# One-hot rows on GpSimd, the last gate product on VectorE and three more early folds there, in a kernel of pooled attention and a top-1 mixture of experts

## The chip, the cores and the metric

The kernel runs on one core of a Trainium2 chip. The time is the device time of one execution in microseconds; of several runs the median is taken. The engines of the core are TensorE (PE in the profile; its weight loads are listed apart as PEld), VectorE (DVE), ScalarE (ACT), GpSimd (POOL) and SyncE (SP, which issues most DMAs). Each works through its own list of instructions in a fixed order and waits at semaphores for the others.

## The reference

Keys and values are averaged over blocks of 8 rows, attention runs over the 72 pooled rows, and its output goes to a top-1 mixture of 8 experts. The shapes are q, k, v of 8 x 8 x 576 x 64; 4608 tokens of width 512; w1 of 8 x 512 x 1024 and w2 of 8 x 1024 x 512; all in float32.

```python
k_p = k.reshape(B, H, Sp, 8, D).mean(axis=3)
v_p = v.reshape(B, H, Sp, 8, D).mean(axis=3)
attn = softmax(q @ k_p.T / sqrt(D))            # + 1e-9 in the denominator
x = (attn @ v_p).transpose(0, 2, 1, 3).reshape(4608, 512)
logits = x @ w_gate + modality_bias[modality_id]
e_idx = argmax(logits); probs = exp(logits - max) / (sum(exp(logits - max)) + 1e-9)
out[t] = probs[t, e_idx] * (relu(x[t] @ w1[e_idx]) @ w2[e_idx])
```

## The kernel before

**Two stages.** The attention (lines 239 to 1059) works through 20 steps, five for each pair of batches: two steps of two 128-token tiles for the even batch, one step of one tile that mixes the leftover 64 tokens of both batches, and two steps for the odd one. That makes 36 tiles, in four groups of 9. The experts follow: tokens are sorted by expert into slots of 256, and each slot runs the two matrix products of its expert. The order on every engine is written out by hand, in the loop over `n` from line 978: what the loop calls first stands first in an engine's list.

**Folding.** A load brings the raw rows of a batch: `k_b` (four chunks of 128 blocks and a rest `k4` of 64) and `v_b` (four pairs of heads and a rest `v4`). Summing the 8 rows of a block is called folding here. GpSimd folds with three additions that halve the width (`fold`, lines 351 to 353); VectorE can fold one chunk with one reduction (`reduce8`, line 356). The results are `kp` and `vp`. TensorE then transposes `kp` (`pk`, line 396; ScalarE copies it to `kt`, lines 404 and 405) and `vp` (`pv`, lines 443 and 444).

**The gate.** The logits of the gate are linear in the values, so 8 extra columns of the value operand `vw` carry `v_p @ w_gate` (`v_gate`, lines 459 to 466): three products on TensorE, two copies by ScalarE, and for the rest `vp4` a copy `vg4` by ScalarE (line 465) and a product with a mask by GpSimd (line 466). The head part of that rest, line 438, is also GpSimd's.

**A step.** TensorE makes the scores `sc` (line 601, or 595 for a mixed tile); VectorE takes their maximum (`mx`, 608) and subtracts it (`sb`, 611); ScalarE takes the exponential (`pe`, 623 and 624). In the next step TensorE transposes the weights (`pp`, 630; the rest in line 642, into a free corner of a score bank) and multiplies them with the values (`a_pe`, lines 665 and 669, into `av`, which has one buffer). VectorE divides by the row sums (`x_dve`, lines 688 to 698: `r`, `lg`, `xb`), and `av` is free again. SP stores `xb` to `xs` in DRAM.

**Routing.** After each group, `route(g)` makes a list of small VectorE operations: logits `lgr`, their maximum, the exponentials `ex` (by ScalarE, 755), the one-hot choice `oh` (760), the sum `sm` of `ex` (777), plus 1e-9 (778), its reciprocal `gate` (782); then a count on TensorE (`pe`, 767 to 771), from which VectorE works out each token's rank, `rk`, `rki`, `rkm`, `rkf`, `rh` (800 to 805), and a row `arow` for each tile, which compares 0 to 127 with the rank (807). The list is dripped: `gap` pops one or two operations between those of a step. The operations that TensorE runs are held back and released once in a step. After group 1, `early_table` multiplies the 18 rows `arow` of groups 0 and 1 with `b0` (line 858, the product) and gets the list of tokens for the first two slots, which GpSimd gathers (line 144). The last group's operations are spread over the first slots of the experts by the table `late` (line 1202).

What order does at the head of a step is told by these lines:

```python
loads(n)
run(hook_0, n)                 # pool_v / pool_k of a coming batch, route
if old: t_pe(old[0]); t_act(old[0]); s_act(n, 0)
s_pe(n, 1)
if due: release()              # one held operation
...
run(hook_1, n)                 # k_operand, v_operand
a_pe(old[0])
s_dve(n, 1)
```

Below, `k_5` means the key rows of batch 5, and "group 1's sum" means the operation `sm` of `route(1)`.

## Time and profile before

| | |
|---|---|
| median of 3 runs | 590.27 us (589.53 to 592.23) |
| the profiled execution | 593.54 us, of which the span is 591.8 us |
| granted clock of TensorE | 0.998 of full |
| TensorE, VectorE, ScalarE, GpSimd busy over the span | 571.0, 370.2, 273.9, 191.8 us |
| folds on GpSimd, lines 351 to 353 | all before 138 us |
| one-hot rows on VectorE, line 807 | 36, between 85.6 and 196.1 us |

All times inside the execution count from the start of the span. A row of the timeline has the start, the busy time, the engine and line, the operation, what it writes and reads, the shapes, how many were merged, and in brackets how long the engine sat idle just before and what ended that. The view of windows lists for a stretch the busy time of PE, PEld, DVE, ACT and POOL (with the number of instructions), the granted clock, the share of the DMA engines and the rate in GB/s. The experts begin at about 184 us.

### The profile page before, as it was taken

The page shows a single profiled execution, that of the slowest core. Times are in us where ns is not written, and L with a number is a line of the kernel's source. Part 1 is how long each engine was busy: PE and PEld are TensorE (multiplying, and loading weights), DVE is VectorE, ACT ScalarE, POOL GpSimd, SP SyncE. Part 2 cuts the span into 40 slices and gives each one's busy share as a digit, 9 for nine tenths or more (in the row PEclk, how much of TensorE's full clock was granted, in tenths as well). Part 3 has the DMA queues.
Part 4 walks back from the last instruction along what each step waited for, and adds up shares of the span by engine and source line. Part 5 has one row for each costly group of instructions (what it writes and reads, how often), then busy time and mean ns, then how long its engine had stood idle before and what let it go on. Part 6 is the DMA issues. An engine that isn't in the chain of part 4 may idle for free.

```text
span 591.8 us, 12343 instructions
## 1 busy us (share of the span) xinstructions
PE 571.0 (96%) x3539; PEld 498.7 (84%) x3539; DVE 370.2 (63%) x941; ACT 273.9 (46%) x653; POOL 191.8 (32%) x300
## 2 busy tenths in 40 slices
PE   4899999999999999999999999999999999999996
PEld 4789889889898888888888888888888888888894
DVE  5757888789876865566455456865455487555311
ACT  2657757788652233334333336633343474334210
POOL 6689996855100233012012112022112113112101
PEclk9999999999999999999999999999999999999999
DMA  8999979994411653332232278232234843241001
GB/s 244 276 336 278 361 235 306 321 314 133 126 56 39 218 210 100 101 112 88 89 113 88 89 225 258 91 118 87 84 122 134 249 168 104 85 148 57 38 3 55
DMA packets 83426, 92.60 MB, mean 156 GB/s; under 512 B 17871, under 2 KB 58319, under 8 KB 83344
## 3 DMA queue, kind: packets, MB, share of 16 engines
q1 hardware_dynamic: 77424, 72.24, 39.4%
q0 software_dynamic: 5920, 19.44, 9.8%
q8 instruction: 30, 0.49, 0.3%
q14 instruction: 52, 0.43, 0.3%
HBM read 123.06 MB, written 27.58 MB: 255 GB/s over the span
## 4 chain that ended last, share of the span: by engine, by line
PE 79%; DMA 7%; DVE 6%; POOL 2%; ACT 2%; issue 2%; SPq 1%; POOLq 0%; DVEq 0%; ACTq 0%
PE op L1335 33%; PE hp L209 20%; PE hp L214 10%; DMA k<-in_k_dram 5%; PE av L665 3%; PE hp L183 3%; PE sc L601 2%; PE av L669 2%; PE ph L183 1%; PE pq L576 1%; PE pp L630 1%; DMA out_dram<-obw,slw 1%; DVE mx L608 1%; DVE hl L141 1%; DVE sb L611 1%
## 5 line engine op out<-in xcount | busy, mean ns | idle before, releaser
L209 PE MATMUL hp<-xhl,hl 128*128 128x512 f32 x512 | 126.6, 389 | 0.0
L1311 POOL DMA_INDIRECT out_dram<-ob,sidx x34 | 36.9, 1084 | 264.0 <-DVE ob L1305 191.5
L209 PEld LDWEIGHTS hp<-xhl,hl 128*128 128x128 f32 x512 | 96.0, 188 | 19.9
L217 ACT COPY ht<-hp 128x256 f32<-128x256 f32 x128 | 47.4, 373 | 139.2 <-PE hp L214 109.9
L218 DVE TENSOR_TENSOR ht<-ht,hp 128x256 f32<-128x256 f32 x128 | 52.7, 420 | 92.0 <-ACT ht L217 83.0
L1335 PE MATMUL op<-hl,hx 128*128 128x512 f32 x429 | 104.7, 392 | 0.0
L1335 PEld LDWEIGHTS op<-hl,hx 128*128 128x128 f32 x429 | 78.4, 188 | 14.6
L1335 PE MATMUL op<-hl,hh 128*128 128x512 f32 x256 | 79.8, 393 | 0.0
L214 PEld LDWEIGHTS hp<-xhl,hl 128*128 128x128 f32 x512 | 69.8, 190 | 4.9
L214 PE MATMUL hp<-xhl,hl 128*128 128x256 f32 x512 | 71.5, 282 | 0.0
L1335 PEld LDWEIGHTS op<-hl,hh 128*128 128x128 f32 x256 | 45.9, 189 | 7.9
L665 PE MATMUL av<-vw,pt 128*128 128x146 f32 (+1 forms) x320 | 49.3, 293 | 1.2 <-DVE xb L698 1.1
L1335 PE MATMUL op<-hl,hlo 128*128 128x512 f32 x128 | 49.8, 389 | 0.0
L144 POOL DMA_INDIRECT xg<-xs,gidx x36 | 38.7, 1074 | 29.0 <-DMA raw<-in_moe_w_dram 13.8
L665 PEld LDWEIGHTS av<-vw,pt 128*128 128x128 f32 (+1 forms) x320 | 39.7, 180 | 3.3 <-DVE xb L698 0.9
L223 DVE SCALAR_TENSOR_TENSOR hx<-ht,hx 128x256 fp32r<-128x256 f32 x64 | 27.1, 425 | 20.4 <-DVEq L1340 15.9
L223 DVE SCALAR_TENSOR_TENSOR hlo<-ht,hh 128x256 fp32r<-128x256 f32 x64 | 27.7, 434 | 18.1 <-DVEq L1340 13.7
L601 PE MATMUL sc<-kt,qt 128*128 128x144 f32 x256 | 37.4, 289 | 1.2 <-ACT qt L582 1.0
L601 PEld LDWEIGHTS sc<-kt,qt 128*128 128x128 f32 x256 | 33.1, 190 | 2.2 <-ACT qt L582 0.9
L608 DVE TENSOR_REDUCE mx<-sc 128x8 f32<-128x576 f32 (+1 forms) x40 | 27.7, 692 | 8.1 <-PE sc L601 6.0
L669 PE MATMUL av<-vw,pt 128*128 128x146 f32 (+1 forms) x160 | 30.1, 290 | 0.3 <-ACT pt L649 0.2
L611 DVE TENSOR_TENSOR sb<-sc,mx 128x576 f32<-128x576 f32 (+1 forms) x40 | 27.7, 693 | 2.4 <-DVE mx L608 0.6
(279 smaller groups left out, 906.5 us busy)
## 6 DMA issues: line engine op xcount, KB each, us to landing
raw<-in_moe_w_dram SPq DMA_DIRECT2D x288, 256.0 KB
xs<-xb SPq DMA_DIRECT2D x16, 528.0 KB
scr<-xg SPq DMA_DIRECT2D x29, 256.0 KB
k<-in_k_dram SPq DMA_DIRECT2D x7, 1024.0 KB
v<-in_v_dram SPq DMA_DIRECT2D x7, 1024.0 KB
q<-in_q_dram SPq DMA_DIRECT2D x7, 1024.0 KB
y<-scr SPq DMA_DIRECT2D x108, 64.0 KB
v<-in_v_dram SPq DMA_DIRECT2D x16, 128.0 KB
```

The costliest lines, as they stand in the source:

```text
L144: nc.gpsimd.indirect_dma_start(out=x, out_offset=None, in_=xs[0:rows, :], in_offset=IndirectOffsetOnAxis(idx[:, col:col + 1].bitcast(U32), 0),
L209: nc.tensor.matmul(hp[g % 2], hl[g][:, 0, d * P:(d + 1) * P], ab[:, d, :, 0:SLOT], start=(d == 0), stop=False)
L214: nc.tensor.matmul(hp[g % 2][:, 0:SLOT], hl[g][:, 1, d * P:(d + 1) * P], ab[:, d, 0, 0:SLOT], start=False, stop=(d == ND - 1))
L217: nc.scalar.copy(hts[g % 2], hp[g % 2][:, SLOT:2 * SLOT])
L218: nc.vector.tensor_add(hts[g % 2], hts[g % 2], hp[g % 2][:, 0:SLOT])
L223: nc.vector.scalar_tensor_tensor(hlo, hts[g % 2], 0.0, hh.bitcast(F32), op0=ALU.max, op1=ALU.subtract)
L601: nc.tensor.matmul(dst, qt[:, i, :], kt[b % NB][:, :, h * SPL:(h + 1) * SPL], start=True, stop=True)
L608: nc.vector.reduce_max(mx, scv, axis=AX.X)
L665: nc.tensor.matmul(av[hs, u, 2 * VC * gg:2 * VC * (gg + 1)], pt[:, c, hs], vw[y][:, c].rearrange("p a x -> p (a x)"), start=(gg == 0), sto ...
L669: nc.tensor.matmul(dst4[hs], pt4[:, hs], v4[y][:, 2 * u:2 * u + 2, :], start=False, stop=True)
L1311: nc.gpsimd.indirect_dma_start(out=out[:, :], out_offset=IndirectOffsetOnAxis(idx.bitcast(U32), 0), in_=ob, in_offset=None, bounds_check=N ...
L1335: nc.tensor.matmul(ot, l[:, ts_], hl[f][:, w, D:2 * D], start=(f == 0 and n == 0), stop=(f == NF - 1 and n == 2))
```

## The change

Five edits:

- **Rows.** GpSimd makes all `arow` rows. A list `onehot` takes those of groups 0 to 2; five of them are issued at the head of a step, ahead of that step's folds. The early product (`joins`) isn't released while rows are left. Group 3's go to GpSimd in the table `late`.
- **Gate product.** `v_gate`'s last product is done by VectorE straight from PSUM; ScalarE's copy `vg4` is gone.
- **Folds.** `k_1` chunk 3 moves later on VectorE; `v_1` chunk 2 and `k_2` chunks 2 and 3 go from GpSimd to VectorE.
- **Order.** In steps 1 and 2 the products `a_pe` move ahead.
- **Sum.** `ex` has a ninth column with 1e-9, set by a GpSimd memset when `route` is called, so that the sum contains it; the addition of line 778 is gone.

```diff
@@ pool_k / pool_v
-                        elif b > 1 or c < 2:
+                        elif b > 2 or c < 2:
                             fold(t[:, c:m], kp[:, c:m])
...
-            elif b:
+            elif b == 2:
                 fold(t[:, 2], vp[:, 2])
-            else:
+            elif b == 0:
                 fold(t[:, 2], vp[:, 2])
                 reduce8(t[:, 3, :], vp[:, 3, :])
...
-        def pool_k_rest(b):
-            reduce8(kraw[b][:, 3, :], kps[b][0][:, 3, :])
+        def pool_k_rest(b, c=3):
+            reduce8(kraw[b][:, c, :], kps[b][0][:, c, :])
...
-        def pool_v_rest(b):
-            reduce8(vraw[b][:, 3, :], vps[b][0][:, 3, :])
+        def pool_v_rest(b, c=3):
+            reduce8(vraw[b][:, c, :], vps[b][0][:, c, :])
@@ v_gate
-            vg4 = ap.tile([P, NPAIR, E], F32, tag="vg4", bufs=1, name=f"vg4_{b}")
-            nc.scalar.copy(vg4, pg[:, 2, :].rearrange("p (j e) -> p j e", j=NPAIR))
-            nc.gpsimd.tensor_tensor(d4[:, :, HD:HD + E], vg4, m4b.to_broadcast([P, NPAIR, E]), op=ALU.mult)
+            nc.vector.tensor_tensor(d4[:, :, HD:HD + E], pg[:, 2, :].rearrange("p (j e) -> p j e", j=NPAIR),
+                                    m4b.to_broadcast([P, NPAIR, E]), op=ALU.mult)
@@ release
-            if drip and drip[0] in held:
+            if drip and drip[0] in held and not (drip[0] in joins and onehot):
                 drip.pop(0)()
+        def some_rows(n):
+
+            for _ in range(min(n, len(onehot))):
+                onehot.pop(0)()
@@ route
-            ex = small("ex", g, [P, n, E])
+            ex = small("ex", g, [P, n, E + 1])
+            nc.gpsimd.memset(ex[:, :, E:E + 1], 1e-9)
...
-                nc.scalar.activation(ex, lg, AF.Exp)
+                nc.scalar.activation(ex[:, :, 0:E], lg, AF.Exp)
...
-            add(lambda: V.tensor_scalar_add(sm, sm, 1e-9))
...
-            for i in range(n):
-                add(lambda i=i: V.tensor_scalar(arow[:, t0 + i, :], iota_b, rkf[:, i:i + 1], None, op0=ALU.is_equal))
+            rows = [lambda i=i: nc.gpsimd.tensor_scalar(arow[:, t0 + i, :], iota_b, rkf[:, i:i + 1], None, op0=ALU.is_equal)
+                    for i in range(n)]
+            if g == len(GROUPS) - 1:
+                ops += rows
+            else:
+                add(lambda: onehot.extend(rows))
@@ early_table
             held.update((count, product))
+            joins.add(product)
@@ the loop over the steps
             loads(n)
+            some_rows(5)
             run(hook_0, n)
...
+            if n == 2:
+                a_pe(old[0])
             run(hook_1, n)
-            if old:
+            if old and n != 2:
                 a_pe(old[0])
             if has:
                 s_dve(n, 1)
-            if n == 1:
-                pool_k_rest(1)
...
+            if n == 1:
+                pool_k_rest(1)
+                pool_v_rest(1, 2)
+                a_pe(old[1])
+                x_dve(old[1])
+            if n == 2:
+                pool_k_rest(2, 2)
             if nxt:
                 s_pe(n + 1, 0)
...
+            if n == 2:
+                pool_k_rest(2)
...
-            if two:
+            if two and n != 1:
                 a_pe(old[1])
-            if two:
                 x_dve(old[1])
...
-        while drip:
+        while drip or onehot:
+            some_rows(GT)
@@ late
-        (0, 0): [lr[9], lr[7], lr[11], lr[8]],
-        (0, 1): [lr[10]],
-        (0, 3): [counts, lr[12]] + [fn for pair in zip(bases, lr[13:20]) for fn in pair] + lr[20:25],
+        (0, 0): [lr[8], lr[7], lr[10]],
+        (0, 1): [lr[9]],
+        (0, 3): [counts, lr[11]] + [fn for pair in zip(bases, lr[12:19]) for fn in pair] + lr[19:],
...
-        (0, 5): lr[25:] + columns,
+        (0, 5): columns,
```

**TensorE in step 1.** Before, the transposes of `kp` of batch 1 (`pk`) are followed by the scores of step 2, which read them, and only then by the value products of the second tile of step 0 (`av`):

```order
L396 MATMUL pk_0_490<-ident,kp_409 64x128 x3
L595 MATMUL sc_0_506<-kt_132,qt_0_481 64x144
L595 MATMUL sc_0_506<-kt_133,qt_0_481 64x144
L595 MATMUL sc_0_506<-kt_132,qt_0_481 64x144
L595 MATMUL sc_0_506<-kt_133,qt_0_481 64x144
L396 MATMUL pk_1_516<-ident,kp_409 64x128
L401 MATMUL pk_1_516<-ident,kp_1_410 64x64
L665 MATMUL av_521<-vw_136,pt_479 128x146 x2
L669 MATMUL av_521<-vw_138,pt_1_135 128x2x73
```

In the changed kernel the same place reads:

```order
L396 MATMUL pk_0_484<-ident,kp_407 64x128 x3
L670 MATMUL av_502<-vw_136,pt_473 128x146 x2
L674 MATMUL av_502<-vw_138,pt_1_135 128x2x73
L670 MATMUL av_502<-vw_136,pt_473 128x146 x2
L674 MATMUL av_502<-vw_138,pt_1_135 128x2x73
L600 MATMUL sc_0_515<-kt_132,qt_0_475 64x144
L600 MATMUL sc_0_515<-kt_133,qt_0_475 64x144
```

The four value products now stand between the transposes and their reader.

**GpSimd after group 0.** Before, the end of the folds of `v_4` is followed by the folds of `k_5`:

```order
L351 TENSOR_TENSOR v_4_758<-v_4_758 128x256
L352 TENSOR_TENSOR v_4_758<-v_4_758 128x128
L353 TENSOR_TENSOR vp_4_1232<-v_4_758 128x64
L351 TENSOR_TENSOR k_756<-k_756 128x2x256
L352 TENSOR_TENSOR k_756<-k_756 128x2x128
L353 TENSOR_TENSOR kp_1350<-k_756 128x128
```

Now:

```order
L351 TENSOR_TENSOR v_4_748<-v_4_748 128x256
L352 TENSOR_TENSOR v_4_748<-v_4_748 128x128
L353 TENSOR_TENSOR vp_4_1218<-v_4_748 128x64
L811 TENSOR_SCALAR arow<-iota_b,rkf_1011 128x128 x5
L351 TENSOR_TENSOR k_746<-k_746 128x2x256
L352 TENSOR_TENSOR k_746<-k_746 128x2x128
```

Five rows of group 0, which read VectorE's `rkf`, stand ahead of the folds of `k_5`; the other four stand ahead of the folds of `v_5`.

**GpSimd at group 1's sum.** Before, the folds of `k_6` end, the two products for the value operand of batch 5 follow, then the folds of `v_6`:

```order
L351 TENSOR_TENSOR k_6_1145<-k_6_1145 64x256
L352 TENSOR_TENSOR k_6_1145<-k_6_1145 64x128
L353 TENSOR_TENSOR kp_6_1591<-k_6_1145 64x64
L438 TENSOR_TENSOR vw_139<-vp_5_1482,m_142 128x4x64
L466 TENSOR_TENSOR vw_139<-vg_5_1719,m_142 128x4x8
L351 TENSOR_TENSOR v_995<-v_995 128x2x256
```

Now:

```order
L351 TENSOR_TENSOR k_6_1131<-k_6_1131 64x256
L352 TENSOR_TENSOR k_6_1131<-k_6_1131 64x128
L353 TENSOR_TENSOR kp_6_1575<-k_6_1131 64x64
L740 MEMSET ex_1589 128x9
L438 TENSOR_TENSOR vw_139<-vp_5_1466,m_142 128x4x64
L351 TENSOR_TENSOR v_983<-v_983 128x2x256
```

The memset of the ninth column, which group 1's sum on VectorE waits for, stands behind all folds of `k_6`. Group 0's stands in the same way behind those of `k_4`.

More of the change, by code (lines that the diff above doesn't have):

```diff
@@ L541 @@
                 tile_group[t] = (g, t - t0)
-        drip, held, stores = [], set(), []
+        drip, held, stores, onehot = [], set(), [], []
         def gap(n=2):
@@ L550, in release @@
         def release():
-            if drip and drip[0] in held:
+            if drip and drip[0] in held and not (drip[0] in joins and onehot):
                 drip.pop(0)()
+        def some_rows(n):
+            for _ in range(min(n, len(onehot))):
+                onehot.pop(0)()
+        joins = set()
         spare, pt4s = {}, {}
```

## The prediction

> **What bounds the kernel now.** I read the page first: TensorE is the busiest engine by far, so the question is where it isn't busy. The view of windows tells that (the first number after the stretch is its length, the second PE's busy time):
>
> ```profile
> 20.00:50.00 30.00, 27.28 (x221) 23.71 (x221) 20.68 (x45) 20.25 (x58) 23.96 (x41) 1.00 1.03 293
> 50.00:112.00 62.00, 60.45 (x506) 55.58 (x505) 51.86 (x155) 42.30 (x120) 52.61 (x91) 1.00 0.98 316
> 112.00:184.00 72.00, 69.92 (x610) 65.19 (x609) 56.94 (x171) 50.76 (x128) 22.70 (x35) 1.00 0.47 152
> 184.00:576.00 392.00, 392.00 (x2063) 336.22 (x2062) 226.49 (x548) 152.44 (x333) 76.60 (x77) 1.00 0.38 121
> ```
>
> From 184 us to 576 us TensorE is busy for 392.00 of 392 us, with the clock at 1.00, and the change takes nothing from its work. So the experts can neither gain nor lose, as long as every operand is there in time. Between 20 and 184 us 2.72, 1.55 and 2.08 us are missing: 6.35 us is all that a change to the attention can win behind the first loads. The timeline of TensorE names its waits; these seven rows are those that the edits touch, or that limit them (times from the span's start, in brackets the idle time and what ended it):
>
> ```profile
> 27.63 0.70 PE L595 MATMUL sc<-kt,qt 128*64 128x144 f32 x6 [0.65 <-ACT kt L405]
> ...
> 33.23 0.30 PE L444 MATMUL pv<-ident,vp 128*64 128x128 f32 x1 [0.81 <-POOL vp L353]
> ...
> 45.72 0.60 PE L576 MATMUL pq<-ident,q 128*128 128x128 f32 x4
> ...
> 48.67 0.30 PE L443 MATMUL pv<-ident,vp 128*128 128x128 f32 x1 [0.47 <-DVE vp L356]
> ...
> 86.99 0.30 PE L642 MATMUL sc<-ident,pe 128*128 128x128 f32 x1 [0.49 <-DVE sb L611]
> ...
> 124.70 0.30 PE L642 MATMUL sc<-ident,pe 128*128 128x128 f32 x1 [0.49 <-DVE sb L611]
> ...
> 165.90 0.66 PE L630 MATMUL pp<-ident,pe 128*128 128x128 f32 x4 [0.54 <-DVE h L187]
> ```
>
> The reader should see three kinds. Early on TensorE waits for `kt`, which is made from `kp`, and for folded values (`vp`), first from GpSimd, then from VectorE. At 86.99 and 124.70 it waits for a VectorE that is busy with one-hot rows of groups 0 and 1. At 165.90 it waits for VectorE among the rows of group 2. The row at 45.72, the transposes of the first queries of `q_2`, has no wait now; it matters below. In all, 0.65 + 0.81 + 0.47 + 0.49 + 0.49 + 0.54 = 3.45 us.
>
> **First term, 20 to 50 us.** The moved value products fill the wait at 27.63; with one fold less and no gate product ahead, GpSimd has `vp4` ready for 33.23. So TensorE comes up to 1.46 us earlier to 45.72. There the load of `q_2` stops it:
>
> ```profile
> 34.37 1.27 POOL L351 TENSOR_TENSOR k<-k 128x512 f32<-128x512 f32 x1 [1.20 <-DMA k<-in_k_dram]
> ...
> v<-in_v_dram SPq DMA_DIRECT2D x1, 1024.0 KB
> k<-in_k_dram SPq DMA_DIRECT2D x1, 1024.0 KB
> q<-in_q_dram SPq DMA_DIRECT2D x1, 1024.0 KB
> v<-in_v_dram SPq DMA_DIRECT2D x2, 128.0 KB
> k<-in_k_dram SPq DMA_DIRECT2D x1, 128.0 KB
> ...
> 34.37:45.72 11.35, 11.06 (x99) 10.06 (x97) 6.80 (x19) 5.97 (x17) 10.56 (x18) 1.00 1.06 335
> ```
>
> `k_2` lands at 34.37, since the fold that waits for it starts then. Behind it in SP's order lie a `k4` of 128 KB, a `v` of 1024, two halves of `v4` of 128 each, a `k` of 1024, and then `q_2` with 1024: 3456 KB, or 3.54 MB. The stretch moves 335 GB/s with the DMA engines full (share 1.06), so they take 10.56 us and `q_2` lands at 34.37 + 10.56 = 44.93, a bit less if the first bytes overlapped `k_2`. TensorE can't win more than 45.72 - 44.93 = 0.8 us there. Meanwhile VectorE, whose scores for step 4 stand ahead of those transposes, catches up, and the wait of 0.47 at 48.67 goes: **+1.3 us** by 50 us. The edits cost VectorE folds:
>
> ```profile
> 36.93 0.73 POOL L351 TENSOR_TENSOR k<-k 128x256 f32<-128x256 f32 x1
> ...
> 40.16 0.72 POOL L351 TENSOR_TENSOR k<-k 64x256 f32<-64x256 f32 x1
> ...
> 73.18 0.61 POOL L438 TENSOR_TENSOR vw<-vp,m 128x256 f32<-128x256 f32 x1
> ...
> L466 POOL TENSOR_TENSOR vw<-vg,m 128x32 f32<-128x32 f32 x8 | 1.9, 237 | 11.5 <-ACT vg L465 11.5
> ...
> L342 POOL MEMSET wgb<- 128x64 f32 x1 | 0.1, 149 | 0.0
> ...
> 47.46 1.07 DVE L356 TENSOR_REDUCE vp<-v 128x64 f32<-128x512 f32 x1
> ...
> 71.08 0.21 DVE L777 TENSOR_REDUCE sm<-ex 128x9 f32<-128x72 f32 x1
> ```
>
> A fold by VectorE takes 1.07 us. Three are new (the fourth is only moved), and VectorE is busy for 20.68 of 30 us in that window. The one that waits for `k_2` at 34.37 has only the maxima of step 3 behind it, for which the scores come later. So I cost them at nothing; without that cover each would cost up to its 1.07.
>
> **Second term, 50 to 75 us.** GpSimd folds without a pause from 34.37 to the row at 73.18. Two chunks of `k_2` go (36.93 to 40.16: 3.23 us), and two gate products at 0.2. So what stood at 73.18 stands at 69.5, and just there stands now the memset of group 0's ninth column. A memset of 64 columns took 149 ns: done at 69.7. Group 0's sum stood at 71.08 on VectorE, with the 1.3 us won at 69.8. The memset is just in time; more than 71.08 - 69.7 = 1.4 us can't be kept at this place. The addition that goes and the gate product that comes on VectorE are both small here and I set them against each other: **0**.
>
> **Third term, 75 to 112 us.** GpSimd's new rows need a price, and no row of the trace shows one. The nearest:
>
> ```profile
> L352 POOL TENSOR_TENSOR k<-k 128x128 f32<-128x128 f32 x12 | 5.5, 456 | 0.9
> ...
> L523 POOL TENSOR_SCALAR mq<-mf 128x36 f32<-128x36 f32 x2 | 0.6, 312 | 0.1
> ...
> L499 POOL TENSOR_SCALAR_AFFINE_SELECT tri<-tri 128x128 bf16<-128x128 bf16 x1 | 0.3, 292 | 0.1
> ```
>
> Two inputs of the same 128 columns take 456 ns, a bf16 operation with one input 292, the same operation with 36 columns 312. I take 0.35 us a row, nearest to the one-input rows, with 0.29 and 0.46 as the ends. [...]
>
> VectorE loses two rows ahead of the `sb` that TensorE waits for at 86.99: +0.5. But GpSimd now waits for VectorE's `rkf` before the folds of `k_5`, and everything behind them is late. When is `rkf` ready?
>
> ```profile
> 83.64 0.72 DVE L802 TENSOR_SCALAR rkm<-rki 128x9 int32<-128x9 int32 x1
> ...
> 84.47 0.44 DVE L804 CAST rkf<-rkm 128x9 f32<-128x9 int32 x1
> ...
> 163.28 0.17 DVE L802 TENSOR_SCALAR rkm<-rki 128x9 int32<-128x9 int32 x1
> ...
> 163.56 0.16 DVE L804 CAST rkf<-rkm 128x9 f32<-128x9 int32 x1
> ```
>
> Before, it ended at 84.91. In group 2, with GpSimd idle, the same `rkm` and `rkf` took 0.17 and 0.16 us in place of 0.72 and 0.44; GpSimd will stand still here. So 84.91 - 0.83 - 1.3 = 82.8. From there GpSimd has nine rows, the folds of `k_5` (as long as those of `k_6`), line 438 at 0.6, the folds of `v_5` and of `k_6`, and then group 1's memset:
>
> ```profile
> 93.27 1.27 POOL L351 TENSOR_TENSOR v<-v 128x512 f32<-128x512 f32 x1
> ...
> 100.09 1.27 POOL L351 TENSOR_TENSOR k<-k 128x512 f32<-128x512 f32 x1
> ...
> 107.49 0.61 POOL L438 TENSOR_TENSOR vw<-vp,m 128x256 f32<-128x256 f32 x1
> ...
> 108.64 0.22 DVE L777 TENSOR_REDUCE sm<-ex 128x9 f32<-128x72 f32 x1
> ```
>
> That is 7.40 + 0.6 + 6.82 + 7.40 + 0.15 = 22.4 us and nine rows: the memset is done at 82.8 + 22.4 + 3.15 = **108.3**. Group 1's sum stood at 108.64 and would now come at 106.8. It waits 1.5 us, with the maxima, `sb` and `x_dve` of step 12 queued behind it, and TensorE behind those. What is left at this point is 108.64 - 108.3 = 0.3, in general 3.5 us minus nine times the price: 0.9 at 0.29, -0.6 at 0.46.
>
> **Fourth term, 112 to 140 us.** The wait of 0.49 at 124.70 goes with group 1's rows: +0.5. But the early product now stands one step earlier, right behind the count at 133.08, and needs group 1's last four rows:
>
> ```profile
> 121.35 0.72 DVE L803 TENSOR_SCALAR rki<-rki 128x9 int32<-128x9 int32 x1
> 121.98 0.16 DVE L804 CAST rkf<-rkm 128x9 f32<-128x9 int32 x1
> ...
> 133.08 0.17 PE L852 MATMUL sc<-cum,ones 128*128 128x8 bf16 x1
> ```
>
> `rkf` ended at 122.14; 0.55 less for `rki` (GpSimd idle then) and 0.3 won: 121.3. Behind it are nine rows, the folds of `k_7` and line 438: 121.3 + 3.15 + 8.0 = 132.4. TensorE arrives at 133.08 - 0.8 = 132.3: no wait at 0.35, but 1.2 us at 0.46. The folds of `v_7`, the gathers and group 2's memset follow; GpSimd is busy for only 22.70 of 72 us in this window, which hides them.
>
> **Fifth term.** The rows of group 2 leave VectorE:
>
> ```profile
> 164.44 0.41 DVE L807 TENSOR_SCALAR arow<-iota_b,rkf 128x128 bf16<-128x128 bf16 x2
> ```
>
> Two of them, 0.4 us, stood ahead of the operation that TensorE waits for at 165.90: +0.3 of 0.54. Group 3's rows go from VectorE to GpSimd in the first slot, where TensorE is full in both: 0. The wider sum and the exponentials written with a gap I cost at nothing to 0.05 each. SP's load of the first expert's index moves ahead of `q_5`'s load; its input comes earlier too: 0.
>
> **Sum:** 1.3 won by 50 us, cut to 0.3 at 112, + 0.5 + 0.3 = **1.1 us** off the profiled execution's 593.54 (its span 591.8 and 1.7 around): 592.4. That execution is 3.3 us above the median of the runs, 590.27; carried over, **589.2**.
>
> **The rivals.**
>
> *GpSimd becomes the bound (slower).* Same mechanism, place 108.64 and 133.08, dearer row. At 0.41 us a row the third term is -0.2, the product waits 0.7, and -0.2 + 0.5 - 0.7 + 0.3 = -0.1: from there on the kernel is slower. At 0.46 it is -0.6 + 0.5 - 1.2 + 0.3 = -1.0 us, 591.3. For it speaks that every fold of GpSimd behind 82.8 is a two-input row at full price; against it the row of 292 ns. [...] Chance 0.25.
>
> *The waits go and nothing takes their place (faster).* If `rkf` comes sooner or a row costs well under 0.29, the sum of group 1 doesn't wait, and of the 3.45 us above all but the capped part goes: 1.3 + 0.5 + 0.5 + 0.3 = 2.6 us, 587.7; with the rest of the touched waits 3.4 us, 586.9. Chance 0.25.
>
> *Hidden anyway.* TensorE's 0.8 us before `q_2` doesn't come, since ScalarE's copies behind the transposes end last, and group 1 takes back the rest: -0.3 to 0.3, 590.3. Chance 0.1.
>
> **How the numbers follow.** The forecast has 0.4 and its own range is 588.3 to 590.0. With the rivals' ends 586.9 to 591.8 (0.5 beyond the dear row, as the product may wait for more), which leaves out 2 in 10 with the scatter of the runs. 0.5%, about what a measurement of this kernel can tell from no change, is 2.95 us: under 587.3 lies half of the faster rival and a little, 0.17; over 593.2 the tail of the slower one, 0.07; between them 0.76.
>
> **What would show it.** Right, if in the changed kernel TensorE's first queries of `q_2` wait for their DMA near 44.9; the waits for `kt` at 27.63 and for `vp` at 33.23 and 48.67 are gone; GpSimd idles for some 5 us until about 82.8 with VectorE's `rkf` as the releaser; VectorE waits for GpSimd at group 1's sum near 108.3; and the waits at 86.99 and 124.70 are gone. Wrong, if rows on GpSimd take over 0.41 us or under 0.29, if `q_2` lands earlier than 44, or if TensorE in step 12 doesn't follow VectorE so closely that a late sum delays it.

## The result, and the profile after

The changed kernel is slower: 597.06 us (594.82 to 600.67, 8 runs) against 592.1 us of the kernel before beside it (8 runs), a ratio of 1.0093 with a 95% interval of 1.0071 to 1.0115. (A ratio is estimated from the single runs, so it need not be the quotient of the two medians.) The forecast was 589.2 us, and its range ended at 591.8.

First the second profile of the kernel before (taken with the experiments below), since the first one was a late execution. The rows are from TensorE's timeline: the transposes of the first queries of `q_2`, at 45.72 in the first profile, and the first 24 products of the experts.

```profile
43.90 0.60 PE L576 MATMUL pq<-ident,q 128*128 128x128 f32 x4
...
181.62 5.72 PE L1335 MATMUL op<-hl,h 128*128 128x512 f32 x24
```

Now the timeline of TensorE in the profile after: the same two rows, and between them the waits that are new.

```profile
42.34 0.63 PE L581 MATMUL pq<-ident,q 128*128 128x128 f32 x4
...
68.66 0.71 PE L600 MATMUL sc<-kt,qt 128*64 128x144 f32 x8 [1.31 <-DVE vw L464]
...
99.63 0.33 PE L443 MATMUL pv<-ident,vp 128*128 128x128 f32 x1 [0.37 <-POOL vp L353]
101.25 0.30 PE L444 MATMUL pv<-ident,vp 128*64 128x128 f32 x1 [1.29 <-POOL vp L353]
...
110.05 0.71 PE L600 MATMUL sc<-kt,qt 128*64 128x144 f32 x8 [2.26 <-DVE vw L464]
...
135.59 0.18 PE L867 MATMUL sc<-b,arow 128*128 128x8 bf16 x1 [0.39 <-POOL arow L811]
136.16 0.18 PE L867 MATMUL sc<-b,arow 128*128 128x8 bf16 x1 [0.39 <-POOL arow L811]
136.74 0.18 PE L867 MATMUL sc<-b,arow 128*128 128x8 bf16 x1 [0.39 <-POOL arow L811]
...
186.28 5.67 PE L1355 MATMUL op<-hl,h 128*128 128x512 f32 x24
```

At 24 us the two profiles are level (the same products start at 24.21 and 24.19). At `q_2` the changed kernel is 43.90 - 42.34 = 1.56 us ahead; at the experts it is 186.28 - 181.62 = 4.66 us behind, which is nearly all of the 4.96 us between the medians and of the 4.71 us between these two executions. So the early folds did what they were meant to, and 6.2 us went between 42 and 186 us. The rows show where: 1.31 + 2.26 us for the bank of the mixed tiles' scores (a bank is here a buffer of the kernel's tile `sc` in PSUM; the gate's products and the scores take turns in it), 0.37 + 1.29 = 1.66 for the folds of `v_5`, 3 x 0.39 = 1.17 in the early product. A fifth loss is no wait. The windows of the same profile, right behind the longest of these waits (the third figure from the end is the granted clock):

```profile
20.00:50.00 30.00, 28.88 (x240) 25.79 (x238) 25.11 (x56) 21.78 (x58) 23.02 (x40) 1.00 1.01 309
50.00:112.00 62.00, 56.36 (x473) 51.98 (x473) 47.63 (x141) 39.11 (x108) 52.10 (x88) 0.99 0.96 316
112.00:184.00 72.00, 69.17 (x592) 64.12 (x590) 53.23 (x151) 49.81 (x125) 34.88 (x53) 0.98 0.44 140
184.00:576.00 392.00, 392.00 (x2070) 335.08 (x2069) 225.42 (x541) 152.85 (x333) 82.38 (x86) 1.00 0.38 121
...
110.00:112.00 2.00, 1.95 (x16) 1.74 (x17) 1.62 (x6) 1.88 (x6) 1.84 (x4) 0.80 1.06 373
112.00:114.00 2.00, 2.00 (x10) 2.00 (x9) 0.00 (x0) 1.13 (x3) 1.84 (x3) 0.50 0.95 285
114.00:116.00 2.00, 2.00 (x16) 1.99 (x15) 1.26 (x5) 0.84 (x3) 1.79 (x4) 0.84 0.28 32
```

TensorE counts as busy there, at half its clock: 2 x (0.20 + 0.50 + 0.16) = 1.72 us are lost. Together 8.1 us; the waits that went (the two of 0.49 for `sb`, and those for `xb`, which fell from 1.6 to 1.1 us in the list of waits) and some waits that shrank behind these make up the rest.

Who made TensorE wait? The timelines of GpSimd and VectorE after:

```profile
67.57 0.11 POOL L740 MEMSET ex<- 128x9 f32 x1
...
81.18 2.92 POOL L811 TENSOR_SCALAR arow<-iota_b,rkf 128x128 bf16<-128x128 bf16 x5 [6.19 <-DVE rkf L809]
...
92.09 2.32 POOL L811 TENSOR_SCALAR arow<-iota_b,rkf 128x128 bf16<-128x128 bf16 x4
94.39 1.27 POOL L351 TENSOR_TENSOR v<-v 128x512 f32<-128x512 f32 x1
...
108.53 0.11 POOL L740 MEMSET ex<- 128x9 f32 x1
...
67.71 0.24 DVE L783 TENSOR_REDUCE sm<-ex 128x9 f32<-128x81 f32 x1 [0.54 <-POOL ex L740]
...
108.67 0.24 DVE L783 TENSOR_REDUCE sm<-ex 128x9 f32<-128x81 f32 x1 [2.52 <-POOL ex L740]
...
109.81 0.18 DVE L464 TENSOR_TENSOR vw<-sc,m 128x32 f32<-128x32 f32 x1
```

GpSimd stands still for 6.19 us until `rkf` comes, with the folds of `k_5` behind it, makes five rows in 2.92 us and four in 2.32, and is late with `v_5` and with group 1's memset. VectorE stands at the sum for 2.52 us, and behind the sum waits the gate product (`vw`, line 464), which reads the bank that TensorE's next scores need. One chain runs through three of the five edits, the rows, the sum and the gate product. The experiments take it apart.

### The profile page after: what moved, and what is told of

Read it like the earlier page. It is cut to its first block, busy times and chain, and to the rows that moved or that the text cites. A ratio compares the mean times of both kernels' runs of the same rounds, so it can differ in the third digit from the quotient of the medians.

```text
span 594.9 us, 12321 instructions
## 1 busy us (share of the span) xinstructions
PE 572.2 (96%) x3539; PEld 499.4 (84%) x3539; DVE 367.1 (62%) x912; ACT 273.5 (46%) x645; POOL 209.4 (35%) x323
## 4 chain that ended last, share of the span: by engine, by line
PE 79%; POOL 7%; DVE 6%; DMA 4%; issue 1%; SPq 1%; ACT 0%; POOLq 0%; DVEq 0%
PE op L1355 33%; PE hp L209 20%; PE hp L214 10%; PE av L670 4%; PE hp L183 3%; PE sc L606 2%; POOL k L351 2%; PE av L674 2%; DMA v<-in_v_dram 2%; POOL k L352 1%; DMA xs<-xb 1%; PE ph L183 1%; POOL arow L811 1%; DVE hl L141 1%; PE pp L635 1%
## 5 line engine op out<-in xcount | busy, mean ns | idle before, releaser
L209 PE MATMUL hp<-xhl,hl 128*128 128x512 f32 x512 | 128.2, 392 | 0.0
L670 PE MATMUL av<-vw,pt 128*128 128x146 f32 (+1 forms) x320 | 50.1, 297 | 1.1 <-DVE xb L703 1.1
L144 POOL DMA_INDIRECT xg<-xs,gidx x36 | 40.0, 1111 | 16.1 <-issue 9.5
L811 POOL TENSOR_SCALAR arow<-iota_b,rkf 128x128 bf16<-128x128 bf16 x36 | 22.6, 644 | 32.4 <-DVE rkf L809 29.7
L674 PE MATMUL av<-vw,pt 128*128 128x146 f32 (+1 forms) x160 | 30.6, 294 | 0.1
```

Source lines behind the costliest of these rows:

```text
L144: nc.gpsimd.indirect_dma_start(out=x, out_offset=None, in_=xs[0:rows, :], in_offset=IndirectOffsetOnAxis(idx[:, col:col + 1].bitcast(U32), 0),
L209: nc.tensor.matmul(hp[g % 2], hl[g][:, 0, d * P:(d + 1) * P], ab[:, d, :, 0:SLOT], start=(d == 0), stop=False)
L670: nc.tensor.matmul(av[hs, u, 2 * VC * gg:2 * VC * (gg + 1)], pt[:, c, hs], vw[y][:, c].rearrange("p a x -> p (a x)"), start=(gg == 0), sto ...
L674: nc.tensor.matmul(dst4[hs], pt4[:, hs], v4[y][:, 2 * u:2 * u + 2, :], start=False, stop=True)
L811: rows = [lambda i=i: nc.gpsimd.tensor_scalar(arow[:, t0 + i, :], iota_b, rkf[:, i:i + 1], None, op0=ALU.is_equal) for i in range(n)]
```

## The experiments

Every ratio is to the kernel before on the same chip. Medians of before were 592.34, 592.72, 592.42 and 592.24 us in the four sets.

### Two profiles more

The kernel before again. No edit.

> The kernel before, unchanged, for a second profile of it. Theory S (scatter): the profile of before that the prediction used was a late one (593.54 us, the medians lie at 590 to 592); a second profile has TensorE's transposes of q_2's first queries, at 45.72 in the first, 1 us or more earlier, and of the 3.5 us of lead that the folds and the order seemed to give, only 2 or less are theirs. Otherwise it comes within 0.3 us of the first profile there.

One time, 591.99 us; `q_2` at 43.90 (above), 1.8 us earlier than in the first profile. Theory S holds: the late start of the first profile is scatter, and comparisons below use this one. (The other profile, of folds and order alone, stands with that kernel.)

### One part of the change undone

**Rows back on VectorE** (groups 0 to 2).

```diff
-            rows = [lambda i=i: nc.gpsimd.tensor_scalar(
+            E_ = nc.gpsimd if g == len(GROUPS) - 1 else V
+            rows = [lambda i=i: E_.tensor_scalar(
...
-            if g == len(GROUPS) - 1:
-                ops += rows
-            else:
-                add(lambda: onehot.extend(rows))
+            ops += rows
```

> The changed kernel with the rows of groups 0 to 2 on VectorE again; all else stays changed. Theory Q (GpSimd's order): nine rows of about 0.58 us, which wait for VectorE's rkf in front of folds that are ready, make the folds of v_5 and group 1's memset late, and the slow clock behind that stall and the late product follow. Then of the changed kernel's waits those for vp at 99.3 and 100.0 (0.5 and 1.5 us), the one behind group 1's sum at 107.9 (2.4), the half clock behind it (1.7) and the product's (1.7) all go, the one behind group 0's sum at 67.4 (1.5, no row stands ahead of it) stays, and the two waits of 0.5 for sb come back: 597.1 - 7.8 + 1.0 = 590.3, within 1 us. Theory M (the memset's place alone): group 1's sum still waits over 1.5 us and the clock still drops: some 594.5. Theory N (the early folds are worth nothing): 592 or above.

595.62 us, ratio 1.0051 (1.0027 to 1.0076): neither 590.3 nor, quite, 594.5. The waits for `v_5` and in the product went, as theory Q said, but TensorE's timeline has others in their place:

```profile
69.64 0.71 PE L600 MATMUL sc<-kt,qt 128*64 128x144 f32 x8 [1.42 <-DVE vw L464]
...
91.75 0.77 PE L670 MATMUL av<-vw,pt 128*128 128x146 f32 x4 [1.34 <-DVE xb L703]
94.45 1.25 PE L606 MATMUL sc<-kt,qt 128*128 128x144 f32 x8 [0.50 <-DVE vw L464]
111.16 0.71 PE L600 MATMUL sc<-kt,qt 128*64 128x144 f32 x8 [0.85 <-DVE vw L464]
...
132.76 0.77 PE L670 MATMUL av<-vw,pt 128*128 128x146 f32 x4 [1.35 <-DVE xb L703]
```

Those at 91.75, 94.45 and 132.76 stand in neither profile of before, though VectorE makes the same rows there. They led to theory C below. The memset of group 1 came at 107.09 although no row stood ahead of it on GpSimd, since `kp` has one buffer and its folds waited 5.92 us for TensorE; but VectorE, slowed as well, reached the sum only at 109.80 and did not wait for it. So in this run the memset's place costs at group 0 alone, where the sum waited 0.54 us.

**Memset early** (in the terms part of step 5, ahead of the folds of `k_4`).

```diff
+        exs = [ap.tile([P, GT, E + 1], F32, name=f"ex_{g}") for g in range(len(GROUPS) - 1)]
...
+            for t in exs:
+                G.memset(t[:, :, E:E + 1], 1e-9)
...
-            ex = small("ex", g, [P, n, E + 1])
-            nc.gpsimd.memset(ex[:, :, E:E + 1], 1e-9)
+            if g < len(GROUPS) - 1:
+                ex = exs[g]
...
```

> The changed kernel with the ninth columns of groups 0 to 2 set once, ahead of the folds of k_4 at about 59 us, in three buffers of their own; rows stay on GpSimd. Theory Q: both waits behind the sums go (1.5 and 2.4 us) and with them the half clock (1.7); TensorE then comes 1.2 us earlier to the folds of v_5, so that the wait there grows from 2.0 to about 3, and the product still waits 1 to 2 us: 597.1 - 5.6 + 1.2 = 592.7. Theory M: the 5.6 us come back in full, nothing else waits more: 591.5 or less. If it is neither, and the waits for the score bank behind the gate product (line 464) stay above 1 us, it is the gate product on VectorE (theory G).

595.05 us, 1.0049 (1.0019 to 1.0079): 2.0 us better than the changed kernel by the medians (the two intervals overlap), of 4.4 to 5.6 expected. The waits at 110 went altogether, 0.59 and 0.98 are left near 70, those for `v_5` (0.39 and 1.29) and the product (three of 0.40) stayed; and now the clock fell behind the product, from 135 to 139 us (0.98 on the mean from 112 to 184 us). So the memset is a part, and the slow clock shows behind another cluster of waits.

**Gate product as before.**

```diff
-            nc.vector.tensor_tensor(d4[:, :, HD:HD + E], pg[:, 2, :].rearrange("p (j e) -> p j e", j=NPAIR),
+            vg4 = ap.tile([P, NPAIR, E], F32, tag="vg4", bufs=1, name=f"vg4_{b}")
+            nc.scalar.copy(vg4, pg[:, 2, :].rearrange("p (j e) -> p j e", j=NPAIR))
+            nc.gpsimd.tensor_tensor(d4[:, :, HD:HD + E], vg4,
                                     m4b.to_broadcast([P, NPAIR, E]), op=ALU.mult)
```

> The changed kernel with the gate's last product as before: ScalarE's copy from PSUM and GpSimd's product. Theory G (TensorE waits only because the bank of its next scores is read by VectorE behind the waiting sum): the waits at 67.4 and 107.9 go altogether, the clock stays at 1.00: 597.1 - 5.6 = 591.5. Theories Q and M: VectorE still stands at the sum with sb and xb queued behind it, so the wait only moves some 1.4 us of TensorE work further, to the value products that wait for xb: 0.1 to 0.5 left at group 0, about 1 at group 1, the clock may stay: 592.5 to 595.

598.13 us, 1.0087 (1.0058 to 1.0117), no better than the changed kernel and above what any of the theories gave. The wait only moves, as Q and M said: 0.42 at 67.69, 0.45 for `sb` and 1.31 for `xb` at 70.92 at group 0, 1.52 for `sb` at 112.28 at group 1. The clock did not stay: it fell behind group 0's waits (0.85, 0.50 and 0.80 in the windows of 2 us from 70 us on). Theory G falls for the changed kernel.

**Only folds and order** (rows, gate product and sum as before; the diff is that of these two edits in the change).

> The kernel before with only the early folds on VectorE and the order of steps 1 and 2; rows, gate product and sum as before. In the changed kernel's profile TensorE is 3.5 us ahead of the profile of before at 36 us, of which 1.5 stood already at 20 us, ahead of every edit that matters, and may be scatter of the start. Theory Q: 2 us of lead are real and nothing on GpSimd takes them, since its queue holds no row and no memset: 592.1 - 2 = 590.1, TensorE busy for about 29 of 30 us between 20 and 50 us. The forecast's cap by the load of q_2: a gain of 1.3 at most, 590.8. Theory N: 592.1 within 0.5.

593.1 us, 1.0007 (0.9986 to 1.0028): no difference by the median, though the profiled execution took 590.17. Hence a second profile of it:

> The kernel with the early folds and the order alone, once more, for a second profile. Its twelve times lie in two heaps, 590.2 to 592.3 and 593.9 to 595.2, and the first profile fell in the lower. Theory K (clock): the upper heap has a stretch of some 3 us at half the clock behind a stall, so that a profile at 594 shows one, with the mean clock at 0.996 or less. Theory L (loads): it has TensorE waiting some 3 us for a load in the first 50 us, with the clock as in the first profile.

It took 591.86 us, in the lower heap again, with the clock at 0.998, so that neither K nor L was put to the test by it. Its waits are those of the first: some 2 us between 67 and 72 us. The mean clocks of the twelve runs lean to K, but only for a part: the six of the upper heap have 0.995 or 0.996, those of the lower 0.996 to 0.999. A difference of about 0.002 is worth 1.2 us of 590, and the heaps lie some 3 us apart; the rest is open.

**Rows and memset undone** (both diffs above; folds, order and gate product are left).

> The changed kernel with the rows of groups 0 to 2 on VectorE and the ninth columns set early, so that of the change the folds, the order, the gate product and the sum are left. Theory C (company): in the run with the rows on VectorE they took 0.53 us on the mean and 1.1 us beside GpSimd's folds, against 0.32 in the kernel before, where GpSimd stood idle for 4 us at the same place, waiting for the copy vg; the gate product on VectorE took that pause away, so the waits behind the rows (0.65, 1.5, 0.7 near 84 to 94 us, 0.7 and 1.5 near 125 to 131) stay and only those behind the sums (1.6 and 1.0) go: 595.6 - 2.6 = 593.0. Theory Q alone (the queue of rows and the memset are all that costs): level with the run of folds and order, 593.1, less the addition, but with rows of 0.32 us and none of the five waits.

597.18 us, 1.0072 (1.0042 to 1.0102), and the five waits of theory C are there: 0.49 at 83.27, 1.35 at 90.06, 0.50 at 92.76, 0.50 at 124.22 and 1.35 at 131.00 (the first and the fourth, for `sb`, stand in the kernel before too). The time is worse than either theory's; the mean clocks of its runs go from 1.000 (594.1 us) to 0.992 (599.6). So with folds and order alone as the base, the gate product, with the sum, costs 4 us. With the rows on GpSimd the time was 595.05, but the two intervals overlap: whether the rows there take a part of that back, these runs can't tell.

**Rows behind the folds of their step** (and the memset early).

```diff
-            some_rows(5)
             run(hook_0, n)
+            some_rows(5)
```

> The changed kernel with the ninth columns set early and each step's rows behind that step's folds instead of ahead of them; all rows on GpSimd. Theory Q1 (it is the standing still for rkf ahead of ready folds): GpSimd's 6.2 us of idle time before 81 us go, the wait for v_5's folds (0.6 and 1.5 us with the memset early) goes, and the product waits for rows that come some 5 us later, but is itself released later: 595.05 - 2.0 = 593.0, and 591.4 if the product's waits (1.7) go too. Theory Q2 (nine rows of 0.58 are 5.2 us of GpSimd wherever they stand): the wait for v_5 stays above 1 us, 594.5 or more.

597.05 us, 1.0091 (1.0055 to 1.0127). The wait for `v_5` is gone, as Q1 said. Its folds end at 100.52, 1.8 us earlier than with the memset alone moved (102.29), so the standing still is a part of what made `v_5` late; but TensorE also came to them 4.4 us later (104.44 against 100.06), which would have hidden the wait by itself. The product now waits 2.76 and three times 0.39 us for rows, and the clock falls twice (0.50 near 74 and near 140 us) in the profiled execution, which took 601.74 us. What the queue gives at one end it takes at the other.

### One part of the change alone, on the kernel before

**The gate product alone.**

> The kernel before with only the gate's last product on VectorE, straight from PSUM. Theory C (company): GpSimd no longer stands still 4 us for the copy vg, so that its folds run beside VectorE's rows of groups 0 and 1, whose mean goes from 0.32 to about 0.5 us; TensorE then waits 1.5 and 0.7 us for xb and the bank near 92 and 133 us: 592.5 + 3.5 = 596. Theory G0 (it costs VectorE three instructions of 0.18 us and nothing else): 592.5 within 0.5.

597.49 us, 1.0076 (1.0048 to 1.0104). Eight instructions of 0.18 us, one for each batch, cost 5 us. The profiled execution is the slowest of the six (602.58 us; the clock fell to 0.50 from 74 to 77 us, and again near 140 us, with 0.98 on the mean from 112 to 184 us), so its waits and places are read here, and not its time. The timelines of VectorE and GpSimd with it:

```profile
70.00 2.11 DVE L777 TENSOR_SCALAR sm<-sm 128x9 f32<-128x9 f32 x1
72.03 0.44 DVE L610 TENSOR_TENSOR sb<-sc,mx 128x288 f32<-128x288 f32 x1
72.40 0.17 DVE L464 TENSOR_TENSOR vw<-sc,m 128x32 f32<-128x32 f32 x1
...
90.27 2.28 DVE L806 TENSOR_SCALAR arow<-iota_b,rkf 128x128 bf16<-128x128 bf16 x2
...
70.26 0.61 POOL L438 TENSOR_TENSOR vw<-vp,m 128x256 f32<-128x256 f32 x1
70.83 1.25 POOL L351 TENSOR_TENSOR v<-v 128x512 f32<-128x512 f32 x1
...
90.50 0.61 POOL L438 TENSOR_TENSOR vw<-vp,m 128x256 f32<-128x256 f32 x1
91.08 1.25 POOL L351 TENSOR_TENSOR v<-v 128x512 f32<-128x512 f32 x1
```

And the same operations in the second profile of before:

```profile
69.51 0.33 DVE L778 TENSOR_SCALAR sm<-sm 128x9 f32<-128x9 f32 x1
...
86.41 1.06 DVE L807 TENSOR_SCALAR arow<-iota_b,rkf 128x128 bf16<-128x128 bf16 x2
...
88.14 0.24 DVE L807 TENSOR_SCALAR arow<-iota_b,rkf 128x128 bf16<-128x128 bf16 x1
88.41 0.20 DVE L807 TENSOR_SCALAR arow<-iota_b,rkf 128x128 bf16<-128x128 bf16 x1
...
91.24 0.24 POOL L466 TENSOR_TENSOR vw<-vg,m 128x32 f32<-128x32 f32 x1 [3.99 <-ACT vg L465]
```

An addition of nine columns takes 2.11 us and ends at 72.11, with GpSimd's fold (72.08), in place of 0.33. Two rows take 2.28 us beside GpSimd's folds, and 0.20 to 0.24 each where GpSimd stands still. Before, GpSimd waited 3.99 us for `vg` at the rows, and those of 0.20 to 0.24 us fall into that pause. At the addition there is no such pause in either kernel: in the one before it met a short add of GpSimd (in the first profile the add ended at 71.63 and the addition at 71.66), and here a product and a long add. That part is a matter of how the two queues happen to lie.

**The rows alone.**

> The kernel before with only the rows of groups 0 to 2 on GpSimd. Theory Q: the two waits of 0.5 for sb and 0.3 in group 2 go, but with rows of 0.58 us behind a wait for rkf the folds of v_5 end some 3 us later, for which TensorE waits about 1 us, and the product waits 1 to 2: 592.5 - 1.3 + 2.5 = 593.7, and 1.7 more in runs in which the clock falls to half. The prediction's terms with its price of 0.35: 592.5 - 1.0 = 591.5.

595.21 us, 1.0046 (1.0026 to 1.0067). TensorE waits 0.54 and 1.31 us for the folds of `v_5` (at 102.17 and 103.82) and 0.23 and three times 0.39 in the product, without any lead from the early folds. The time is above theory Q's 593.7 and 3.7 us above what the prediction's own terms give with its price of a row (591.5).

**The ninth column alone.**

> The kernel before with only the ninth column: its memset when a group's routing begins, so behind the folds of that step, and no addition. Theory M: group 0's sum, at 71.08 before, waits for a memset at about 73.3 behind the folds of k_4, 2.2 us less 0.3 for the addition; TensorE waits about as long; group 1's memset at 107.5 comes in time: 592.5 + 1.9 = 594.4. The prediction's slack (1.4 us were there, and nothing is lost): 592.5 within 0.5.

596.22 us, 1.0062 (1.0039 to 1.0084). From VectorE's timeline:

```profile
72.14 0.24 DVE L778 TENSOR_REDUCE sm<-ex 128x9 f32<-128x81 f32 x1 [2.14 <-POOL ex L735]
```

This is theory M's mechanism, at more than its 594.4 us: group 0's sum waits 2.14 us for the memset, and TensorE 1.95 and 1.31 us behind it; then the clock falls (0.76, 0.50 and 0.89 in the three windows of 2 us from 74 us on), which costs 1.7 us more. Group 1's sum, at 111.94, does not wait.

### What in the gate product costs, and what makes a row dear

**The pause restored.** The copy and GpSimd's product stay, into a tile that nothing reads; the real product is VectorE's.

```diff
+            nc.vector.tensor_tensor(d4[:, :, HD:HD + E], pg[:, 2, :].rearrange("p (j e) -> p j e", j=NPAIR),
+                                    m4b.to_broadcast([P, NPAIR, E]), op=ALU.mult)
             vg4 = ap.tile([P, NPAIR, E], F32, tag="vg4", bufs=1, name=f"vg4_{b}")
...
-            nc.gpsimd.tensor_tensor(d4[:, :, HD:HD + E], vg4, m4b.to_broadcast([P, NPAIR, E]), op=ALU.mult)
+            nc.gpsimd.tensor_tensor(vx4, vg4, m4b.to_broadcast([P, NPAIR, E]), op=ALU.mult)
```

> The kernel before with the gate product on VectorE from PSUM, and beside it ScalarE's copy and GpSimd's product as before, into a tile that nothing reads: GpSimd pauses for vg as before, the bank waits for VectorE. Company: VectorE's rows take about 0.32 us on the mean again, the waits for xb and the bank near 94 and 136 us (1.5 and 0.7 each) go, the addition is short: 593, within 1. Bank: the waits of TensorE's next scores for line 464 (3.1 and 2.1 us with the gate product alone) stay above 1.5: 595.5 or more.

**The bank by ScalarE.**

```diff
-            nc.gpsimd.tensor_tensor(d4[:, :, HD:HD + E], vg4, m4b.to_broadcast([P, NPAIR, E]), op=ALU.mult)
+            nc.vector.tensor_tensor(d4[:, :, HD:HD + E], vg4, m4b.to_broadcast([P, NPAIR, E]), op=ALU.mult)
```

> The kernel before with ScalarE's copy vg4 kept and only the product on VectorE, from the copy: the bank is given back by ScalarE as before, and GpSimd has no pause. Company: rows of about 0.5 us, waits near 94 and 136 us as with the gate product alone, the addition above 1 us: 596 to 597.5. Bank: level with before, 592.5 to 593.5.

594.08 us, 1.0026 (1.0008 to 1.0044), with the pause, and 598.46 us, 1.0113 (1.0082 to 1.0143), without it. VectorE's rows, grouped by form (busy time, mean ns of one, idle before), first with the gate product alone:

```profile
L806 DVE TENSOR_SCALAR arow<-iota_b,rkf 128x128 bf16<-128x128 bf16 x36 | 15.3, 459 | 0.0
```

With the pause restored:

```profile
L810 DVE TENSOR_SCALAR arow<-iota_b,rkf 128x128 bf16<-128x128 bf16 x36 | 10.3, 322 | 0.0
```

With the bank given back by ScalarE:

```profile
L807 DVE TENSOR_SCALAR arow<-iota_b,rkf 128x128 bf16<-128x128 bf16 x36 | 15.3, 461 | 0.0
```

And GpSimd's pause at the rows of group 0, and TensorE at the bank of the first mixed tile behind group 0, with the pause restored:

```profile
91.83 0.24 POOL L469 TENSOR_TENSOR vx<-vg,m 128x32 f32<-128x32 f32 x1 [4.82 <-ACT vg L467]
...
70.21 0.71 PE L598 MATMUL sc<-kt,qt 128*64 128x144 f32 x8 [1.00 <-ACT vg L467]
```

It is the company. Both times lie a little above the ranges given (594 and 597.5), but the order is that of theory company, and the rows have their old time exactly where GpSimd has its pause. A copy on ScalarE and a product on GpSimd more, both for nothing, make the kernel 597.49 - 594.08 = 3.4 us faster than the gate product alone, and 598.46 - 594.08 = 4.4 us faster than the version without the pause. Not all of the 3.4 is the pause's: at group 0's sum GpSimd pauses in neither, and there the addition took 0.33 us in place of 2.11 and TensorE waited 1.00 us in place of 2.96. What the pause does not bring back is 594.08 - 592.24 = 1.8 us. TensorE's waits for the bank, 1.00, 0.44 and 0.43 us, where the kernel before has none of 0.2 or more, are as much; two of them are for the copy that is there for nothing. One point missed: with the bank by ScalarE the addition stayed short (0.23 us on the mean of four), so not every such operation is caught.

**Rows from float32.**

```diff
-nc.gpsimd.tensor_scalar(arow[:, t0 + i, :], iota_b, rkf[:, i:i + 1], None, op0=ALU.is_equal)
+nc.gpsimd.tensor_scalar(arow[:, t0 + i, :], iota_f, rkf[:, i:i + 1], None, op0=ALU.is_equal)
```

> The changed kernel with the rows compared from the float32 iota in place of the 16-bit one. If the 16-bit input makes a row dear: 0.45 us or less in place of 0.64. If it is the form (a comparison with a scalar of each partition): 0.6 and more as before, and the time as that of the changed kernel.

GpSimd's rows, grouped by form, in this kernel:

```profile
L811 POOL TENSOR_SCALAR arow<-iota_f,rkf 128x128 bf16<-128x128 f32 x36 | 22.6, 645 | 32.7 <-DVE rkf L809 30.0 <-DVE rh L810 2.7
```

And in the changed kernel:

```profile
L811 POOL TENSOR_SCALAR arow<-iota_b,rkf 128x128 bf16<-128x128 bf16 x36 | 22.6, 644 | 32.4 <-DVE rkf L809 29.7 <-DVE rh L810 2.7
```

596.53 us in one run. The type of the input does nothing (645 against 644 ns); that it is the form (a scalar for each partition) is what is left, and wasn't tried by itself.

### A version without what costs

Folds and order, the memset early in place of the addition, and on GpSimd only the rows of group 2; gate product and the other rows as before. The lines for the rows (the others stand above):

```diff
+            E_ = nc.gpsimd if g == EARLY_GROUPS else V
+            rows = [lambda i=i: E_.tensor_scalar(arow[:, t0 + i, :], iota_b, rkf[:, i:i + 1], None, op0=ALU.is_equal)
+                    for i in range(n)]
+            if g == EARLY_GROUPS:
+                add(lambda: onehot.extend(rows))
+            else:
+                ops += rows
```

> The early folds and the order, the ninth columns set early in place of the addition, and the rows of group 2 alone on GpSimd, which has nothing else to do there; gate product and rows of groups 0 and 1 as before. With the folds and the order alone TensorE waits 0.34, 0.82 and 0.79 us near 67 to 70 us, where the addition took 0.90 us on VectorE, and 0.69 at 162. Theory: the first three shrink by 0.9 and the last by 0.5, so 593.1 - 1.4 = 591.7; if the upper heap of the times of that kernel is the half clock behind these three waits, it goes too: 590.3. If the heaps have another cause, 591.7 or above.

590.37 us (588.47 to 591.45, 12 runs), 0.9967 (0.9951 to 0.9984): 0.3% less than the kernel before, a little but clear of the noise, and less than the changed kernel. From its timelines, TensorE at `q_2`, near 70 us and at the experts, and GpSimd's nine rows:

```profile
42.97 0.63 PE L585 MATMUL pq<-ident,q 128*128 128x128 f32 x4 [0.40 <-DMA q<-in_q_dram]
...
67.97 0.71 PE L604 MATMUL sc<-kt,qt 128*64 128x144 f32 x8 [0.38 <-ACT vg L465]
69.81 0.74 PE L674 MATMUL av<-vw,pt 128*128 128x146 f32 x4 [0.44 <-DVE xb L707]
...
179.55 5.68 PE L1363 MATMUL op<-hl,h 128*128 128x512 f32 x24
...
160.35 6.31 POOL L819 TENSOR_SCALAR arow<-iota_b,rkf 128x128 bf16<-128x128 bf16 x9 [13.82 <-DVE rkf L816]
```

The experts begin 181.62 - 179.55 = 2.07 us earlier than before, as much as the medians differ (2.05). At `q_2` it is 43.90 - 42.97 = 0.93 us ahead, which is the folds' and the order's; the rest comes behind, where the addition and group 2's rows have left VectorE. How the gain would divide without the folds, no run shows. The time is that of the expectation's second branch (590.3), but no profile of the upper heap shows whether its reason, the clock, is the right one.

## Why the prediction was wrong

**The first term came out in its sum, but not by its parts.** 1.3 us were forecast by 50 us: 0.8 at `q_2`, under a cap by its load, and the wait of 0.47 at 48.67. At `q_2` alone 1.56 came. The cap exists (TensorE waits 0.40 us for that load in the last experiment, 0.58 with the gate product as before and 1.83 with the rows behind the folds), but in the profile after it didn't bind. And of the three early waits the last stayed: TensorE still waits 0.46 us for VectorE's fold at 45.11. That the sum is near is in part luck.

**The step that failed is the third term's price of a row.** 0.35 us was taken, "nearest to the one-input rows", with 0.29 and 0.46 as the ends. A row took 0.64 us, five of them 2.92 (0.58 from start to start): outside the ends; none of the rows that they came from has this form. With 0.58 in the prediction's own formulas, the third term is 3.5 - 5.2 = -1.7 and the product waits 121.3 + 5.2 + 8.0 - 132.3 = 2.2: the sum is -1.7 + 0.5 - 2.2 + 0.3 = -3.1 in place of 1.1. That is 4.2 of the 6.1 us between 1.1 won and 5.0 lost; and the rows alone, which the prediction's terms make 1.0 us faster, were 2.8 us slower. That is the rival "GpSimd becomes the bound", which turned at 0.41 and was given 0.25; its price and its range ended too soon. Undoing the rows in the changed kernel brought back only 1.4 us by the medians, since on VectorE they met GpSimd's folds without the old pause (534 ns on the mean, against 321 in the second profile of before).

**The base was low as well.** The forecast started from 590.27, the median of three runs; that of eight is 592.1. So 1.8 of the 7.9 us between forecast and time lie there, and not in the change.

**Two consumers were left out.** The sum of GpSimd's queue was compared with group 1's memset alone; the folds of `v_5`, which stand ahead of the memset, cost TensorE 1.66 us first. And behind VectorE's sum not only the maxima and `sb` are queued, but the gate product, which holds TensorE's next bank. The second of these sets only where TensorE waits: with the gate product as before, the wait moved to `sb` and `xb`, and the time stayed.

**The second term, "0", was wrong twice.** Group 0's memset was to be just in time, by 1.4 us of slack at the most. In the changed kernel VectorE waited 0.54 us for it. TensorE waited 1.31 us behind it, of which the memset explains only that part: TensorE came to the bank 2.3 us earlier than before (67.35 against 69.67), VectorE to the sum only 1.6 us earlier (67.71 against 69.26), and the gate product now stands between. With the ninth column alone, without the early folds, VectorE waited 2.14. And the gate product was set against the addition as "both small". By its duration it is; by its place it costs 5.1 us alone. In the change itself that is not seen in this form, since the rows that suffer from it have left VectorE.

**What was right:** GpSimd stands still for `rkf`, VectorE waits at group 1's sum, and the two waits for `sb` are gone. The times were reckoned on the first profile, which runs 1.8 us later than the second (45.72 against 43.90); on the clock of the second, GpSimd's idle time was forecast to end at 81.0 and the memset at 106.5. The one ended at 81.18, the other at 108.64: 2.1 us late, and nine times the 0.23 us by which a row was underpriced from start to start are 2.07. Of the fifth term's 0.3 half came: TensorE's wait for `h` fell from 0.53 to 0.38 us.

**The slow clock wasn't in the sum at all.** 1.72 us in the profile after, and by the mean clocks of its eight runs (0.990 in the one of 600.67 us, 0.998 in the one of 594.82) none to three such losses (an estimate: 1.72 us of a span of 594.9 are 0.003 of the mean clock). That the waits bring it on is read from the profiles, where each stretch follows a cluster of waits; no run tried the clock by itself, and the same waits do not always bring it (last section).

The edits don't add: alone, the gate product, the rows and the ninth column cost 5.1, 2.8 and 3.8 us, folds and order 0.8 (no measurable difference), together 5.0. The profiles fit that: with the rows on GpSimd TensorE waits for `v_5` and in the product, with the rows on VectorE beside the gate product it waits for `xb`, so one loss takes the other's place.

## What to carry to other kernels

Price an instruction by its form on its engine, and when no row shows the form, put the rival's price well beyond the nearest rows. Before an instruction joins an engine's queue, list everything that is queued behind it, and who waits for each (here GpSimd stood still for 6.19 us at its first rows, with the folds of `k_5` behind them). Ask what fills a pause that an edit removes: without GpSimd's pause of 3.99 us VectorE's rows took 459 ns on the mean in place of 321 (the gate product alone). And count the clock beside the waits: behind 3.9 us of waits in the changed kernel and 3.3 us with the ninth column alone, 1.7 us of clock were lost in each of the two profiled executions, and behind the waits of the changed kernel none in that with the rows from float32.

## What the runs showed of the hardware

**VectorE's short operations beside GpSimd's adds.** An addition of nine columns took 0.16 us at the shortest (at 109.14 in the first profile of before), and 0.33 and 2.11 where it ended within 0.03 us of an add of GpSimd (71.66 and 71.63 in that profile; 72.11 and 72.08 with the gate product alone). A row took 0.20 to 0.24 us with GpSimd idle (88.14 to 89.32 in the second profile of before), and 1.1 to 1.2 us beside its longest adds (two in 2.28 at 90.27, one in 1.19 at 93.75, with the gate product alone). Those adds took 1.27 us on the mean in the first profile of before and 1.26 with the gate product alone. `cum`, a sum of two inputs of 8 columns, took 0.10 us with GpSimd idle (at 152.74 in the first profile of before), and 0.59 and 0.89 where it ended within 0.03 us of a product or an add of GpSimd (73.82 and 73.79 in that profile; 74.68 and 74.65 with the gate product alone). Not every short operation is caught: the addition of 0.16 us began 0.01 us behind the start of a long add (109.13). What holds VectorE up there, no view shows.

**Half the clock, in some executions, behind waits of 0.4 to 2.3 us.** In the changed kernel, after 2.26 us without work (and 1.66 us some 9 us earlier), TensorE lost 1.72 us of clock, with a lowest of 0.50 from 112 to 114 us; with the ninth column alone 1.7 us after waits of 1.95 and 1.31, with 0.50 from 76 to 78 us. The changed kernel with the rows from float32 has the same waits at the same place (0.36 and 1.29, then 2.26 us), and there it kept its clock:

```profile
110.00 0.71 PE L600 MATMUL sc<-kt,qt 128*64 128x144 f32 x8 [2.26 <-DVE vw L464]
...
112.00:114.00 2.00, 2.00 (x18) 2.00 (x18) 0.89 (x5) 1.57 (x3) 1.84 (x3) 1.00 1.09 366
```

In that execution (mean clock 0.996) the clock fell later, to 0.50 at 136 us, behind three waits of some 0.4 us in the early product. What decides between the two is open.
